# Long convolution and MLP on one core: v of the last two channel blocks fetched in the transform's layout, tables of the inverse transform read as a constant

## The chip, the core and the metric

The kernel runs on one core of one Trainium2 chip. The core has five engines with an instruction queue each: TensorE (PE, whose weight loads the profile shows as PEld), VectorE (DVE), ScalarE (ACT), GpSimd (POOL) and SyncE (SP, which here only issues DMAs). The metric is the device time of one execution in microseconds (us), as the median of several runs. Everything is float32; the MLP's products are done as sums of split operands.

## The reference

```python
mod = (silu(c) @ w_mod).reshape(1, 6, 1, 640)            # sa, ca, ga, sb, cb, gb
h  = layernorm(x) * (1 + ca) + sa                        # x is A_q, 2048 x 640
k_shift[s] = sum_t k[s - t] * shift_k[:, t]              # causal, 4 taps, by channel
kv = k_shift * v
y  = irfft(rfft(kv, 4096) * rfft(ssm_k, 4096))[:2048]    # long causal convolution by channel
y  = y + kv * ssm_D
x  = x + ga * (h * y)
h  = layernorm(x) * (1 + cb) + sb
x  = x + gb * (relu(h @ w1 + b1) ** 2 @ w2 + b2)         # 640 -> 1728 -> 640
```

## The kernel before

The 640 channels are worked in five blocks b = 0 to 4 of 128 channels. For each block the product x = k_shift * v is made with channels on the partitions, in four quarters h of 512 time steps: `kv_load` fetches 512 rows of k and of v (natural layout, time on the partitions) into one of the `KN` buffers; `kv_k` turns k round with four PE transposes (L223) and starts the sum of taps on ACT; `kv_s` adds the other taps on DVE (L235); `kv_v` turns v round with four transposes (L245) and issues the next `kv_load`; `kv_m` multiplies on DVE (L252) and stores the quarter to `kv_d` in DRAM (L253). When all four quarters are in DRAM, `load_x` (L200) reads them back in the transform's layout: partition (a, n) with a = 0 to 3 and n = 0 to 31, free axes g = 0 to 31 and i = 0 to 63, where the channel is 4g + a and the time step 64n + i. `load_h` (L192) reads ssm_k, the filter, in the same layout into the other half of the same tile `p`. `skip` adds ssm_D to the filter's first sample, so that the convolution gives y + kv * ssm_D; for block 0 it reads the row `d0` on POOL, for the others the table `dsm` on DVE (L139, `p<-p,dsm`).

The transform has these steps. `unit_a` (L360, tiles `pa`): a product along n, 16 units per block, the filter's eight first, then x's eight; ACT copies each unit to `a`. `spectrum` (L367): a product along i with the table `gb`, of the filter (tiles `h`, or `eh` in `early_h` for block 0) and of x. `front(b, j)`, j = 0 to 7: the two spectra, two DVE products of 128 x 512 (L136), two POOL sums (L142, L139). `back(b, j)`, j = 0 to 3 (L433, tiles `qp`): the inverse along i with the table `gi`, from the results of fronts 2j and 2j + 1. `unit_t` (L497) turns the result round, `unit_y` (L508) does the inverse along n and writes y to `up`. The gate and the residual follow on ACT (`prep_a`), DVE (`prep_m`, `gate`, `finish_near`) and POOL (`prep_p`, `finish_add`).

`gb` is read from DRAM as a constant. `gi` is made of it on the chip: `make_gi(i)`, i = 0 to 7, four PE transposes (L334) and a copy to `gi` by DVE or ACT; only its first half plane is read as a constant (L839).

The order is written out by hand. After a prologue (`kv_all`, the filter and x of block 0) there are steps: FS(b, 0 to 9), the spectrum phase of block b, in which eight fronts and four backs run and, at FS(b, 9), the first two `unit_a` of block b + 1; and GS(b, 0 to 17), the rest of block b, beside the other `unit_a` of block b + 1. `at(place, function)` hangs further work on a step: the kv quarters of block b in the steps of block b - 2, loads, the modulation rows (`part_load`, `part_scale`, `part_add`), LayerNorm statistics. `keep_order` fixes this order on every engine, so each queue is served strictly in the order of the program, SP's DMA queue too. An SP DMA also waits for the eighth DMA before it that uses the same semaphore. After block 4 the MLP runs (L680 to L784), and is not touched.

In the profiled execution the prologue lasts to 37.23 us, FS(0) to 64.0, GS(0) to 94.6, FS(1) to 121, GS(1) to 154.8, FS(2) to 178.5, GS(2) to 211.7, FS(3) to 236, and the MLP starts at about 309.

Of the kernel before, what the change touches and what calls it, by code (L numbers as in the profile page):

```python
# [30 lines left out]
def _constants():  # L31
    N = 4096
    n1 = np.arange(64)
    n2 = np.arange(32)
    m = np.arange(32)
    th = 2 * np.pi * ((n2[:, None] * m[None, :]) % 64) / 64
    cr, ci = np.cos(th), -np.sin(th)
    cr[:, 0] = 1.0
    ci[:, 0] = (-1.0) ** n2
    cw = np.zeros((4, 32, 2, 32, 4))  # L40
    for d in range(4):
        cw[d, :, 0, :, d] = cr
# [45 lines left out]
def ssm_mlp_kernel(  # L88
# [40 lines left out]
    def copy(eng, o, i):  # L129
        if eng is act:  # L130
            act.activation(o, i, AF.Copy)  # L131
        else:
            eng.tensor_copy(o, i)
# [45 lines left out]
    dve.memset(dsm, 0.0)  # L179
    tap = sb.tile([P, NB, 4], F32, tag="tap", name="tap")  # L180

    hsrc = ssm_k.rearrange("(g a) (n i) -> (a n) g i", a=4, i=64)
    xsrc = kv_d.rearrange("(g a) (n i) -> (a n) g i", a=4, i=64)
    pt = {}

    def p_tile(b):
        pt[b] = sb.tile([P, 2, DG, 64], F32, tag=f"S{b % 2}", name=f"p_{b}")

    def load_h(b, n=1):
        w = DG // n  # L190
        for i in range(n):
            sp.dma_start(  # L192
                pt[b][:, 1, i * w : (i + 1) * w],
                hsrc[:, b * DG + i * w : b * DG + (i + 1) * w, :],
            )

    def load_x(b, n=1):
        w = DG // n
        for i in range(n):
            sp.dma_start(  # L200
                pt[b][:, 0, i * w : (i + 1) * w],
                xsrc[:, b * DG + i * w : b * DG + (i + 1) * w, :],
            )
# [35 lines left out]
    def kv_v(b, h, tag="X"):  # L239
        t = kt[1] = ps.tile(  # L240
            [P, 512], F32, tag=tag, name=f"vt_{b}_{h}", bufs=4 if tag == "X" else 2
        )
        kn = KN[h % (4 if b == 0 else 2)]
        for j in range(4):
            pe.transpose(t[:, j * P : (j + 1) * P], kn[:, 1, j], ident)  # L245
        n = 4 * b + h + 2
        if 6 <= n < 4 * NB:
            kv_load(n)

    def kv_m(b, h):  # L250
        acc = KACC[h % 2] if b else K0[:, h]
        dve.tensor_mul(acc, kt[1], acc)  # L252
        sp.dma_start(kv_d[b * P : (b + 1) * P, h * 512 : (h + 1) * 512], acc)  # L253
# [70 lines left out]
    def load_gb():  # L324
        src = gb_d.rearrange("p (g r a f) -> p g r a f", g=16, r=2, a=2)
        for i in range(4):
            sp.dma_start(gb[:, 4 * i : 4 * i + 4], src[:, 4 * i : 4 * i + 4])
        sp.dma_start(gi[0:64, 0], gi0_d.rearrange("f (r n) -> f r n", r=2))

    def make_gi(i):  # L330
        t = ps.tile([P, 2, 2, P], F32, tag="T", name=f"git_{i}", bufs=2)
        for u in range(2):
            for r in range(2):
                pe.transpose(t[:, u, r], gb[:, 2 * i + u, r].rearrange("p a f -> p (a f)"), ident)  # L334
        if i == 0:
            copy(dve, gi[64:128, 0], t[64:128, 0])
            copy(dve, gi[:, 1], t[:, 1])
        else:
            copy(act if i % 2 else dve, gi[:, 2 * i : 2 * i + 2], t)
# [161 lines left out]
    def unit_y(b, g):  # L501
        if g % 2 == 0:
            ys[0] = ps.tile([P, 8, NL, 4], F32, tag="Y", name=f"y_{b}_{g}", bufs=2)
        y = ys[0]
        for i in range(4):
            for r in range(2):
                for h in range(2):
                    pe.matmul(  # L508
                        y[64 * h : 64 * h + 64, 4 * (g % 2) + i],
                        tss[g][:, i, 64 * r : 64 * r + 64],  # L510
                        ca[:, r, h],
                        start=(r == 0),
                        stop=(r == 1),
                    )
        if g % 2:
            uo = UPt[b][:, :, 16 * (g - 1) : 16 * (g + 1)].rearrange("p l (g d) -> p g l d", d=4)
# [331 lines left out]
    for a in range(4):  # L848
        pool.dma_start(
            dsm[32 * a : 32 * a + 1, :],  # L850
            ssm_D.rearrange("(o g a) -> a o g", a=4, o=1)[a],
        )
# [8 lines left out]
    def FS(b, j):  # L861
        return 28 * b + j
# [403 lines left out]
```

## Time and profile before

| | |
|---|---|
| median of 3 runs | 713.6 us (713.49 to 715.56) |
| profiled execution | 712.45 us |
| its span (first to last instruction) | 710.6 us |
| mean granted TensorE clock | 0.996 of full |
| instructions | 18542 |
| DVE busy | 339.1 us (48%) |
| ACT busy | 336.2 us (47%) |
| POOL busy | 297.3 us (42%) |
| DMA packets | 88403, 72.64 MB, of them 19392 under 512 B |

The profiled execution is one run of its own, so sums are made against 712.45 us, of which 1.85 us lie outside the span. A row of the timeline reads: start, length (of several merged instructions, from the first start to the last end), engine, line, operation, output<-inputs, count, and in brackets how long the engine sat idle before it and what released it. A row of the chain of waits reads: start, length, what. A row that groups instructions gives their count, busy time and mean length in ns. A row of busy time by window is explained where it is shown.

### The profile page before, as it was taken

How to read it: one execution, taken by the hardware profiler on the slowest of the kernel's cores; microseconds unless marked ns; L12 is line 12 of the kernel's file. 1: busy time of each engine (PE TensorE's matmuls, PEld its weight loads, DVE VectorE, ACT ScalarE, POOL GpSimd, SP SyncE). 2: the span in 40 equal slices, each digit the busy share in tenths (PEclk: the TensorE clock that was granted, in tenths of full speed). 3: DMA queues.
4: the chain of work that ended last, by engine and by line, in shares of the span. 5: the costliest groups of instructions: out<-in, count | busy, mean ns of one | idle time of the engine just before them, and what ended most of it. 6: DMA issues, size and time to landing. Idle time of an engine off the chain costs nothing.

```text
span 710.6 us, 18542 instructions
## 1 busy us (share of the span) xinstructions
PE 691.7 (97%) x7916; PEld 659.7 (93%) x7916; DVE 339.1 (48%) x667; ACT 336.2 (47%) x689; POOL 297.3 (42%) x343
## 2 busy tenths in 40 slices
PE   6899999999999999999999999999999999999997
PEld 5788898889899899789999999999999999999996
DVE  4355674775868679669831222222312313312313
ACT  3535565776884886557523323323333333233221
POOL 3033036157846969842532522422513415325213
PEclk9999999999999999999999999999999999999999
DMA  9787584869555464417320020020020100200101
GB/s 247 207 191 238 156 289 149 250 184 255 138 164 148 112 166 147 116 58 232 103 75 1 1 76 1 1 75 1 9 67 1 44 32 1 75 1 1 38 1 39
DMA packets 88403, 72.64 MB, mean 102 GB/s; under 512 B 19392, under 2 KB 74112, under 8 KB 88320
## 3 DMA queue, kind: packets, MB, share of 16 engines
q1 hardware_dynamic: 86176, 70.83, 34.8%
q8 instruction: 62, 1.02, 0.6%
q10 hardware_dynamic: 1888, 0.60, 0.4%
q14 instruction: 21, 0.17, 0.1%
q0 software_dynamic: 256, 0.01, 0.0%
HBM read 57.02 MB, written 14.42 MB: 101 GB/s over the span
## 4 chain that ended last, share of the span: by engine, by line
PE 90%; DVE 4%; ACT 2%; DMA 2%; issue 1%; POOL 1%; POOLq 0%; DVEq 0%; SPq 0%; ACTq 0%
PE acc L759 26%; PE h L689 25%; PE pa L360 9%; PE y L508 5%; PE qp L433 5%; PE x L367 5%; PE h L367 4%; PE t L497 3%; PE kt L223 1%; PE h L680 1%; PE vt L245 1%; PE xtp L654 1%; DVE KV L235 1%; PE gr L1035 1%; DMA d<-in_A_ssm_D_dram 1%
## 5 line engine op out<-in xcount | busy, mean ns | idle before, releaser
L136 POOL TENSOR_TENSOR mtmp<-mtmp 128x256 f32<-128x256 f32 x112 | 71.8, 641 | 242.2 <-ACT mtmp L721 232.5
L689 PE MATMUL h<-xt,w_S 128*128 128x256 f32 x1290 | 166.9, 281 | 0.2 <-DVE w_S L142 0.2
L689 PEld LDWEIGHTS h<-xt,w_S 128*128 128x128 f32 x1290 | 161.2, 190 | 0.4 <-DVE w_S L142 0.4
L759 PE MATMUL acc<-w_S,hring 128*128 128x320 f32 x960 | 156.8, 311 | 0.2 <-DVE hring L142 0.2
L142 DVE TENSOR_TENSOR hring<-mtmp,hring 128x256 fp32r<-128x256 f32 x112 | 65.1, 581 | 189.6 <-ACT hring L131 189.5
L759 PEld LDWEIGHTS acc<-w_S,hring 128*128 128x128 f32 x960 | 141.8, 188 | 0.7 <-DVE hring L142 0.7
L721 ACT ACTIVATE mtmp<-h,b1t 128x256 f32<-128x256 f32 x104 | 49.3, 474 | 176.6 <-PE h L689 173.6
L360 PE MATMUL pa<-wx,p 128*64 128x128 f32 x1280 | 82.8, 278 | 2.6 <-POOL p L139 1.8
L360 PEld LDWEIGHTS pa<-wx,p 128*64 128x64 f32 x1280 | 69.6, 138 | 9.6 <-issue 4.7
L131 ACT ACTIVATE hring<-mtmp 128x256 fp32r<-128x256 f32 x112 | 46.7, 417 | 45.7 <-POOL mtmp L136 44.2
L131 ACT ACTIVATE a<-pa 128x512 f32<-128x512 f32 x80 | 47.8, 602 | 27.9 <-PE pa L360 27.8
L136 DVE TENSOR_TENSOR wx<-x,wx 128x512 f32<-128x512 f32 x64 | 40.9, 681 | 19.3 <-PE x L367 10.1
L142 POOL TENSOR_TENSOR we<-wx 128x256 f32<-128x256 f32 x20 | 15.9, 794 | 73.5 <-DVE wx L136 69.8
L508 PE MATMUL y<-wx,wx 128*64 128x64 f32 x1280 | 45.0, 225 | 1.5 <-ACT wx L131 0.8
L508 PEld LDWEIGHTS y<-wx,wx 128*64 128x64 f32 x1280 | 41.7, 139 | 4.9 <-issue 2.6
L235 DVE SCALAR_TENSOR_TENSOR KV<-kt,tap,KV 128x511 f32<-128x511 f32 (+2 forms) x48 | 35.6, 743 | 19.0 <-ACT ktail L131 16.3
L139 POOL TENSOR_TENSOR wm<-wm,wm 128x640 f32<-128x640 f32 x20 | 32.0, 1602 | 29.5 <-ACT wm L308 29.3
L656 DVE TENSOR_SCALAR we<-xtp,cbs 128x256 f32<-128x256 f32 x35 | 19.0, 544 | 51.1 <-PE xtp L654 51.0
L367 PE MATMUL x<-a,gb 128*64 128x128 f32 x640 | 41.7, 273 | 0.7 <-ACT a L131 0.7
L131 ACT ACTIVATE q<-qp 128x512 f32<-128x512 f32 (+1 forms) x40 | 21.3, 584 | 36.1 <-PE qp L433 36.1
L367 PEld LDWEIGHTS x<-a,gb 128*64 128x64 f32 x640 | 35.9, 137 | 1.7 <-ACT a L131 0.9
L367 PE MATMUL h<-a,gb 128*64 128x128 f32 x512 | 34.1, 275 | 0.0
(145 smaller groups left out, 1040.5 us busy)
## 6 DMA issues: line engine op xcount, KB each, us to landing
wm<-in_w_mod_dram SPq DMA_DIRECT2D x25, 320.0 KB, 4.7
KV<-in_A_k_dram SPq DMA_DIRECT2D x20, 256.0 KB, 5.4
KV<-in_A_v_dram SPq DMA_DIRECT2D x20, 256.0 KB, 4.5
xp<-in_A_q_dram SPq DMA_DIRECT2D x5, 1024.0 KB, 7.5
out_dram<-x SPq DMA_DIRECT2D x14, 320.0 KB, 2.2
w1s<-in_B_w_dram SPq DMA_DIRECT2D x13, 320.0 KB, 3.7
w2s<-in_B_w_dram SPq DMA_DIRECT2D x13, 320.0 KB, 4.0
kv_d<-KV SPq DMA_DIRECT2D x16, 256.0 KB, 3.6
```

The lines of the kernel that those rows point to most:

```text
L131: act.activation(o, i, AF.Copy)
L136: eng.tensor_mul(o, a, b)
L139: eng.tensor_add(o, a, b)
L142: eng.tensor_sub(o, a, b)
L235: dve.scalar_tensor_tensor(o, x, tap[:, b, t : t + 1], o, op0=ALU.mult, op1=ALU.add)
L360: pe.matmul(t[64 * r : 64 * r + 64, u], w, cw[:, r], start=True, stop=True)
L367: pe.matmul(t[64 * a : 64 * a + 64, s + r], gb[:, g, r, a], AX[b][i][:, 2 * g + a], start=True, stop=True,)
L433: pe.matmul(t[a][:, u], gi[l, 4 * j + u, r], w[r][l, u % 2], start=(r == 0), stop=(r == 1),)
L508: pe.matmul(y[64 * h : 64 * h + 64, 4 * (g % 2) + i], tss[g][:, i, 64 * r : 64 * r + 64], ca[:, r, h], start=(r == 0), stop=(r == 1),)
L689: pe.matmul(hps[n, f][:m], WI[1, f][:, a, b], XT[n][:, x, b], start=(b == 0 and i == 0), stop=(b == NB - 1 and i == 2),)
L721: act.activation(r[:m], h[:m], AF.Relu, bias=b1t[:m, f : f + 1])
L759: pe.matmul(acc[2 * s + i], h[:, a, s * P : (s + 1) * P], w[:, y, i * 320 : (i + 1) * 320], start=(f == 0 and ti == 0), stop=(f == NF - 1 ...
```

## The change

Blocks 3 and 4 (`APART`) take another order of channels: partition (a, n), place g holds channel 32a + g in place of 4g + a. For them `kv_load` fetches k alone, `kv_v` and the DVE product of `kv_m` are gone, and what is stored to `kv_d` is the tap sum of k. v is fetched by `v_load` straight in the transform's layout into four buffers `VB` of 128 x 512 (i, g), that lie where the tap sums and the v halves of `KN` were: 16 DMAs per block, each 32 partitions x 16 steps x 32 channels, that is pieces of 128 B. `x_mul` multiplies them into x in place, four DVE products of 128 x 512 per block, in FS(2, 4 to 7) for block 3 and FS(3, 4, 5, 7, 8) for block 4. `load_x` and `load_h` of these blocks are four DMAs of 32 partitions in place of one. The write of y to `up` places its elements 32 apart in place of four side by side.

`gi` is read from DRAM whole, in four DMAs of 512 KB, and `make_gi` is gone. `early_h` 4 and 5 of block 0 move from FS(0, 0 and 1) into the prologue, 6 and 7 to FS(0, 0 and 1). Of the four `d0` loads two are now issued by ACT. The `dsm` loads become eight POOL DMAs in FS(0, 0 to 3), in place of four in the prologue. `skip` of blocks 1 and 3 moves from step 4 to step 8 of the spectrum phase before. The filter of block 2 is loaded at GS(0, 14) in place of FS(0, 2), that of block 3 at FS(2, 2) in place of FS(2, 0), and `load_xp` of block 1 at FS(2, 7) in place of FS(2, 1).

```diff
+    gb = gb.reshape(128, 16, 2, 2, 64).transpose(0, 1, 3, 2, 4)
+    gt = gb.transpose(3, 4, 1, 2, 0).copy()
+    gt[0, :, 0] = gi.reshape(2, 64, 128).transpose(1, 0, 2)
...
+        "gi": gt.reshape(128, 4096).astype(f),
...
+    APART = (3, 4)
+
+    def by_channel(src, b, i, dst):
+        w = dst.shape[1]
+        if b not in APART:
+            v = src.rearrange("(g a) (n i) -> (a n) g i", a=4, i=64)
+            sp.dma_start(dst, v[:, b * DG + i * w : b * DG + (i + 1) * w, :])
+            return
+        for a in range(4):
+            c = b * P + 32 * a + i * w
+            sp.dma_start(
+                dst[32 * a : 32 * a + 32],
+                src[c : c + w, :].rearrange("g (n i) -> n g i", i=64),
+            )
...
-        for w, src in ((0, k), (1, v)):
+        for w, src in ((0, k),) if b in APART else ((0, k), (1, v)):
...
     def kv_m(b, h):
         acc = KACC[h % 2] if b else K0[:, h]
-        dve.tensor_mul(acc, kt[1], acc)
+        if b not in APART:
+            dve.tensor_mul(acc, kt[1], acc)
         sp.dma_start(kv_d[b * P : (b + 1) * P, h * 512 : (h + 1) * 512], acc)
+    VB = [
+        t.rearrange("p (i g) -> p i g", g=DG)
+        for t in (KV[:, 0:512], KV[:, 512:1024], KV[:, 1536:2048], KV[:, 2560:3072])
+    ]
+
+    def v_load(b, j):
+        src = v.rearrange("(n i) d -> n i d", i=64)
+        for a in range(4):
+            c = b * P + 32 * a
+            sp.dma_start(
+                VB[j][32 * a : 32 * a + 32], src[:, 16 * j : 16 * j + 16, c : c + 32]
+            )
+
+    def x_mul(b, j):
+        x = pt[b][:, 0, :, 16 * j : 16 * j + 16]
+        mul(dve, x, x, VB[j].rearrange("p i g -> p g i"))
...
-    def make_gi(i):
...
+    def load_gi(i):
+        src = gi_d.rearrange("p (g r n) -> p g r n", g=16, r=2)
+        sp.dma_start(gi[:, 4 * i : 4 * i + 4], src[:, 4 * i : 4 * i + 4])
...
+                uo = UPt[b].rearrange("p l (d g) -> p g l d", d=4)[:, 4 * (g - 1) : 4 * (g + 1)]
...
-        pool.dma_start(
+        (pool if a % 2 else act).dma_start(
             d0[32 * a : 32 * a + 1, 0 : D - a], ssm_D[a:D].rearrange("(o d) -> o d", o=1)
...
-    for i in range(2):
-        make_gi(2 * i)
-        make_gi(2 * i + 1)
-        early_h(0, 2 * i)
-        early_h(0, 2 * i + 1)
+    for j in range(6):
+        early_h(0, j)
...
-        at(FS(b - 1, 4), skip, b)
+        at(FS(b - 1, 8 if b in (1, 3) else 4), skip, b)
...
+    for a in range(4):
+        at(FS(0, a), load_dsm, a)
+    for j in range(2):
+        at(FS(0, j), early_h, 0, 6 + j)
...
-    at(FS(0, 2), load_h, 2)
+    at(GS(0, 14), load_h, 2)
...
-        at(FS(2, 0) if b == 3 else GS(2, 1), load_h, b)
+        at(FS(2, 2) if b == 3 else GS(2, 1), load_h, b)
+
+    put_v(3, [FS(2, i) for i in (0, 0, 1, 1)], [FS(2, i) for i in (4, 5, 6, 7)])
+    put_v(4, [FS(3, i) for i in (0, 0, 1, 1)], [FS(3, i) for i in (4, 5, 7, 8)])
...
-    at(FS(2, 1), load_xp, 1)
+    at(FS(2, 7), load_xp, 1)
```

More of the change, by code (lines that the diff above doesn't have):

```diff
@@ L105, in ssm_mlp_kernel @@
     gb_d: bass.AP,
-    gi0_d: bass.AP,
+    gi_d: bass.AP,
     out: bass.AP,
@@ L180, in ssm_mlp_kernel @@
     tap = sb.tile([P, NB, 4], F32, tag="tap", name="tap")
-    hsrc = ssm_k.rearrange("(g a) (n i) -> (a n) g i", a=4, i=64)
-    xsrc = kv_d.rearrange("(g a) (n i) -> (a n) g i", a=4, i=64)
     pt = {}
@@ L191, in load_h @@
         for i in range(n):
[L192 to L195, printed above, removed]
+            by_channel(ssm_k, b, i, pt[b][:, 1, i * w : (i + 1) * w])
     def load_x(b, n=1):
@@ L199, in load_x @@
         for i in range(n):
[L200 to L203, printed above, removed]
+            by_channel(kv_d, b, i, pt[b][:, 0, i * w : (i + 1) * w])
     def kv_load(i):
@@ L245, in kv_v, with kv_next @@
             pe.transpose(t[:, j * P : (j + 1) * P], kn[:, 1, j], ident)
+        kv_next(b, h)
+    def kv_next(b, h):
         n = 4 * b + h + 2
@@ L322, in ssm_mlp_kernel @@
     gi = sb.tile([P, 16, 2, P], F32, tag="S6", name="gi")
[L324 to L328, printed above, removed]
-    def make_gi(i):
[L331 to L339, printed above, removed]
+    def load_gi(i):
+        src = gi_d.rearrange("p (g r n) -> p g r n", g=16, r=2)
+        sp.dma_start(gi[:, 4 * i : 4 * i + 4], src[:, 4 * i : 4 * i + 4])
     AX, QT = {}, {}
@@ L515, in unit_y @@
         if g % 2:
-            uo = UPt[b][:, :, 16 * (g - 1) : 16 * (g + 1)].rearrange("p l (g d) -> p g l d", d=4)
+            if b not in APART:
+                uo = UPt[b][:, :, 16 * (g - 1) : 16 * (g + 1)].rearrange("p l (g d) -> p g l d", d=4)
+            else:
+                uo = UPt[b].rearrange("p l (d g) -> p g l d", d=4)[:, 4 * (g - 1) : 4 * (g + 1)]
             if b < NB - 1:
@@ L809, in load_h0 @@
     def load_h0(i):
-        sp.dma_start(pt[0][:, 1, 8 * i : 8 * i + 8], hsrc[:, 8 * i : 8 * i + 8, :])
+        by_channel(ssm_k, 0, i, pt[0][:, 1, 8 * i : 8 * i + 8])
         skip(0, 8 * i, 8 * i + 8)
@@ L838, in ssm_mlp_kernel, with load_dsm @@
     load_gb(3)
-    sp.dma_start(gi[0:64, 0], gi0_d.rearrange("f (r n) -> f r n", r=2))
     kv_load(4)
+    load_gi(0)
     kv_load(5)
+    load_gi(1)
     load_h(1)
-    for i in range(2):
-        make_gi(2 * i)
-        make_gi(2 * i + 1)
-        early_h(0, 2 * i)
-        early_h(0, 2 * i + 1)
[L848 to L851, printed above, removed]
+    load_gi(2)
+    load_gi(3)
+    for j in range(6):
+        early_h(0, j)
+    def load_dsm(a):
+        pool.dma_start(
+            dsm[32 * a : 32 * a + 1, 0:96],
+            ssm_D[0 : 3 * P].rearrange("(o g a) -> a o g", a=4, o=1)[a],
+        )
+        pool.dma_start(
+            dsm[32 * a : 32 * a + 1, 96:].rearrange("o (c g) -> o c g", g=DG),
+            ssm_D[3 * P :].rearrange("(o c a g) -> a o c g", o=1, a=4, g=DG)[a],
         )
@@ L879, in put_kv, with put_v @@
             at(p4[0], kv_k, b, h, tags[h])
+            if b in APART:
+                at(p4[1], kv_s, b, h)
+                at(p4[1], kv_next, b, h)
+                at(p4[2], kv_m, b, h)
+                continue
             for i, fn in zip(p4[1:], (kv_s, kv_v, kv_m)):
                 at(i, fn, b, h)
+    def put_v(b, ld, mu):
+        for fn, p4 in ((x_mul, mu), (v_load, ld)):
+            for j, i in enumerate(p4):
+                at(i, fn, b, j)
     for b in range(1, NB):
-        at(FS(b - 1, 4), skip, b)
-    for j in range(4):
-        at(FS(0, j // 2), make_gi, 4 + j)
-        at(FS(0, j), early_h, 0, 4 + j)
+        at(FS(b - 1, 8 if b in (1, 3) else 4), skip, b)
[3 more added lines that the diff above has]
+        at(FS(0, j), early_h, 0, 6 + j)
     put_kv(1, [
```

3 lines of the change are left out of this document (1 added, 2 removed).

## The prediction

> **What bounds the kernel now.** I read the page's busy shares and chain first, then busy time by stage, then the rows inside the stages that change. On the page:
>
> ```profile
> PE 691.7 (97%) x7916; PEld 659.7 (93%) x7916; DVE 339.1 (48%) x667; ACT 336.2 (47%) x689; POOL 297.3 (42%) x343
> PE 90%; DVE 4%; ACT 2%; DMA 2%; issue 1%; POOL 1%; POOLq 0%; DVEq 0%; SPq 0%; ACTq 0%
> ```
>
> TensorE is busy for 97% of the span and is 90% of the chain that ends last. A TensorE instruction taken out is therefore worth its time, unless the stage that it stood in has another limit close behind. The busy times by stage show that. Columns: window, its length, busy time of PE, PEld, DVE, ACT, POOL, then granted clock, DMA share, GB/s.
>
> ```profile
> 37.23:64.00 26.77, 26.25 (x385) 22.96 (x385) 17.27 (x30) 9.36 (x18) 11.76 (x18) 1.00 0.78 197
> 121.00:154.81 33.81, 32.98 (x570) 28.68 (x566) 23.23 (x52) 25.87 (x46) 9.28 (x6) 1.00 0.72 205
> 154.81:178.52 23.71, 23.71 (x390) 21.89 (x389) 13.48 (x24) 15.51 (x33) 17.09 (x21) 1.00 1.03 258
> 178.52:211.65 33.13, 32.63 (x586) 29.60 (x586) 27.82 (x53) 28.15 (x60) 21.64 (x16) 1.00 0.54 155
> 211.65:236.05 24.40, 24.40 (x424) 23.18 (x420) 17.60 (x32) 13.06 (x24) 16.98 (x22) 1.00 0.44 121
> ```
>
> These are FS(0), GS(1), FS(2), GS(2) and FS(3). PE is full in all of them. In GS(2), ACT (28.15 of 33.13) and DVE (27.82) are near.
>
> Before 37.23 something else is the limit. The chain in order of time (start, length, what):
>
> ```profile
> 3.51 4.71 DMA d<-in_A_ssm_D_dram
> ...
> 19.86 2.37 DVE kacc L235 x6
> 23.04 2.37 DMA kv_d<-kacc
> ...
> 29.34 7.22 PE pa L360 x128
> ```
>
> The start hangs on d0, and from 19.86 to 29.34 on the product of block 0 and its way through DRAM. TensorE waits there.
>
> **The change part by part.** 64 transposes leave PE: 32 that made `gi` (L334, 8 groups of 4) and 32 of v for blocks 3 and 4 (L245, 8 groups). That they are gone is certain from the order of the instructions. Their price is the distance of starts:
>
> ```profile
> 38.26 0.66 PE L334 MATMUL git<-ident,gb 128*128 128x128 f32 x4
> 38.84 1.09 PE L367 MATMUL eh<-a,gb 128*64 128x128 f32 x16
> ...
> 41.38 1.04 PE L367 MATMUL eh<-a,gb 128*64 128x128 f32 x16
> 42.35 1.09 PE L334 MATMUL git<-ident,gb 128*128 128x128 f32 x8
> 43.79 0.66 PE L223 MATMUL kt<-ident,KV 128*128 128x128 f32 x4 [0.35 <-DVE gi L133]
> ...
> 70.05 0.66 PE L497 MATMUL t<-ident,q 128*128 128x128 f32 x4
> 70.64 1.09 PE L360 MATMUL pa<-wx,p 128*64 128x128 f32 x16
> ...
> 125.78 0.66 PE L245 MATMUL vt<-ident,KV 128*128 128x128 f32 x4
> ...
> 126.80 1.09 PE L360 MATMUL pa<-wx,p 128*64 128x128 f32 x16
> ```
>
> A `gi` group takes 38.84 - 38.26 = 0.58 us, an `early_h` 42.35 - 41.38 = 0.97 at most (0.9 taken, as the two beside each other run closer). A v group stands ahead of a t group: both take 1.02, a t group alone 0.59, so it is worth 0.43.
>
> *Prologue.* Four `gi` groups go and two more `early_h` come, all inside the wait that ends at 29.34: worth 0. But d0 now comes through two POOL and two ACT issues in place of four on POOL. The last POOL issue started at 3.51; now it is the second, two issues earlier, at 0.535 each (the L849 row below): 1.1. The chain starts with it: **+1.1**. At the least it is 0, if the first piece of ssm_k, or ACT's two issues, is what comes last then.
>
> *FS(0).* Four `gi` groups (two alone, 1.16, and two in 42.35 to 43.79, 1.44 with the wait) and two `early_h` (1.8) leave PE: 4.4. What is late next is in these rows:
>
> ```profile
> L849 POOL DMA_DIRECT2D dsm<-in_A_ssm_D_dram x4: 528/535/557, 16.1 to 17.7; - x4
> ...
> 40.50 0.73 POOL L139 TENSOR_TENSOR we<-wx 128x256 f32<-128x256 f32 x1
> ...
> 41.40 0.28 POOL L414 COPY we<-wx 1x128 f32<-1x128 f32 x1
> ...
> 57.73 0.74 DVE L235 SCALAR_TENSOR_TENSOR KV<-kt,tap,KV 128x511 f32<-128x511 f32 x1
> ...
> 59.68 1.97 PE L360 MATMUL pa<-wx,p 128*64 128x128 f32 x32
> ...
> 60.22 1.28 DVE L136 TENSOR_TENSOR wx<-x,hs 128x512 f32<-128x512 f32 x2
> ```
>
> That last row is the eighth front's product. The dsm loads, in four DMAs at 16.1 in an idle POOL, become eight, two behind each of the fronts 0 to 3, 0.535 each. So POOL has 2 x 0.73 + 2 x 0.535 = 2.5 us per front. From 41.7 (end of L414) fronts 1, 2 and 3 are ready at 44.2, 46.7 and 49.3, and the second `qp`, which needs front 3, starts at 49.3 (52.64 before). Then come 2.0 of it, 0.6 of kt and 0.9 of x: x of front 6 is there at 52.8. Behind that DVE has in order front 6 (1.3), the taps of k, quarter 1 of block 1 (60.22 - 57.73 = 2.5), front 7 (1.3), and now skip(1), moved from FS(0,4) to FS(0,8): 58.2. PE's next instruction, pa of block 1, needs skip(1) and could have run at 56.1. It starts at 58.2 in place of 59.68, and with `qp` 3 behind it the stage ends 1.9 earlier (62.1 for 64.0): **+1.9** of the 4.4. The eight DMAs' landing (about 49.3 + 1 + 6) is no later than that. The 2 MB of `gi` on SP's queue stand ahead of the ssm_k of block 1, and lie in the 27 us at 197 GB/s above; they are due at the `qp`s from 44.2 on: 0, and 0 to 2 if they are late.
>
> *GS(1) and GS(2).* Eight v groups: 8 x 0.43 = 3.5. Eight DVE products go too, and 8 of SP's 256 KB loads. In GS(2), 33.1 - 1.7 = 31.4 remain for ACT's 28.15, which is 90% with waits in order: I take off 0.5: **+3.0** (bounds 1 and 3.5).
>
> *FS(2).* Four products of v, 24 DMAs of 32 partitions (x 4, v 16, ssm_k 4; before 2 DMAs) and skip(3) at FS(2,8) meet here:
>
> ```profile
> 150.13 1.54 DVE L235 SCALAR_TENSOR_TENSOR KV<-ktail,tap,KV 128x3 f32<-128x3 f32 x1
> 154.37 0.38 SPq L253 DMA_DIRECT2D kv_d<-KV  x1
> 158.99 0.68 SPq L200 DMA_DIRECT2D p<-kv_d  x1
> 160.12 3.47 SPq L192 DMA_DIRECT2D p<-in_A_ssm_k_dram  x1
> ...
> 171.11 0.22 DVE L139 TENSOR_TENSOR p<-p,dsm 128x32 f32<-128x32 f32 x1 [3.40 <-issue]
> ...
> 175.67 1.27 DVE L136 TENSOR_TENSOR wx<-x,wx 128x512 f32<-128x512 f32 x2
> ...
> 176.62 1.97 PE L360 MATMUL pa<-wx,p 128*64 128x128 f32 x32
> 161.00:169.00 8.00, 8.00 (x140) 7.54 (x138) 3.29 (x6) 4.89 (x10) 6.08 (x8) 1.00 1.13 223
> ```
>
> x and ssm_k, 1 MB each in pieces of 256 B, took from 158.99 to 171.11 (skip(3) waited for the second): 12.1 us. At the 223 GB/s of the last row a load is 4.7 of it, and 2.7 are start and landing. The store waited until 154.37 for the loads ahead of it in the queue and for the product of v; now it can go when the taps end (150.13 + 1.54 = 151.67) and the queue has issued one load, at about 152.2, and x 2.2 us earlier than before, at 156.8. Between the two stands v, 8192 pieces of 128 B. No row has such a piece. Below, at equal bytes per us, it takes 4.7; above, at equal pieces per us, 9.4. I take 7. ssm_k lands at 156.8 + 12.1 + 7 = 175.9 (173.6 to 178.3). SP's 24 issues, at 0.4 each (row 154.37), are under that.
>
> DVE: products with both inputs in SBUF run from
>
> ```profile
> 214.95 0.68 DVE L136 TENSOR_TENSOR up<-up,KV 128x512 f32<-128x512 f32 x1
> ...
> 218.85 2.29 DVE L136 TENSOR_TENSOR up<-up,KV 128x512 f32<-128x512 f32 x1
> ```
>
> 0.68 to 2.29; I take 0.9, nearer the free one, because POOL has gaps between its pairs. The strided v operand is priced as these rows; doubled it would add 0.7. The 3.4 us that DVE lost ahead of 171.11 pay for the first three. Front 7 stays at 175.67; behind it are 1.27, the fourth product 0.9, one more of the gate's rows (0.7) and skip (0.2): 178.7. Block 3's pa wants it at 176.62: a new wait of **-2.0** (bounds 0 and -5). What is queued behind skip(3) on DVE, the gate of block 0, loses nothing that PE waits for.
>
> *FS(3).* The same four products; skip(4) stays early and x, v have from about 212 to 226. Front 7 is late by 0.2: **-0.2**. The strided writes of block 3's and 4's y are priced at 0; the four in GS(3) have 7 us of free DVE, and doubling the last two of block 4 would cost 0.7.
>
> *Clock.* A wait of TensorE has cost a second time here:
>
> ```profile
> 285.00:288.40 3.40, 1.88 (x26) 1.33 (x23) 1.17 (x3) 3.37 (x9) 3.40 (x4) 1.00 0.00 0
> 288.60:292.00 3.40, 3.40 (x32) 3.07 (x31) 3.37 (x5) 2.31 (x4) 3.40 (x3) 0.50 0.00 0
> ...
> 288.41 2.64 PE L497 MATMUL t<-ident,q 128*128 128x128 f32 x12 [1.29 <-ACT q L131]
> ```
>
> After 3.4 us in which PE was busy for 1.88, the granted clock was 0.50 for 3.4 us. Twelve transposes took 2.64 there, against 3 x 0.59 = 1.8; with the y behind them I put such a stretch at 1.3. The change makes three waits of about 2 us (before 29.34 minus 1.1, before skip(1), before skip(3)). I charge one stretch: **-1.3** (bounds 0 and -3.9). [...]
>
> Sum: 1.1 + 1.9 + 3.0 - 2.0 - 0.2 - 1.3 = **2.5 us less**. The profiled execution took 712.45 (span 710.6 and 1.85 around it), so 709.95 by that; it ran 1.15 under the median of 713.6, so I name 713.6 - 2.5 = **711.1**.
>
> **The rivals.** *The clock stays full.* For it: the clock stands at 1.00 in all five stages quoted first, short waits and all. Against: the rows at 285 to 292. Gain 3.8: 709.8.
>
> *No new wait.* If both skips are in time and ACT keeps up, all is gained: 1.1 + 4.4 + 3.5 = 9.0: 704.6. For it is PE at 97%; against it are the two DVE queues counted above.
>
> *Slower: the ssm_k of block 3 is late behind v.* It is one queue, and pa of block 3 waits for its end. The time follows what a piece of 128 B costs: at 1.15 ns (a piece of 256 B: 4.7 us / 4096) DVE is still the later one. The gain is gone when skip(3) comes 2.5 later, v taking about 12 us (1.5 ns a piece); slower by over 0.3% begins near 14.5. At twice a 256-B piece, 18.8, ssm_k lands at 187.7, pa waits 11 in place of 2, and the kernel takes about 720. For it: the pieces are half the size and the DMAs cover 32 partitions. Against: fewer bytes per piece should not take longer. [...]
>
> *Others are the limit already.* ACT in GS(1) and GS(2) and DVE in FS(0) give back the rest: gain 0 to 1, 713. For it: 28.15 busy on ACT; against: PE has hardly an idle row in those stages.
>
> **How the numbers follow.** About 0.3%, 2.1 us, is what a measurement of this kernel can tell from no change. Chances: forecast 0.40 (own range 709.6 to 712.6), clock full 0.20, no new wait 0.12, v late 0.15, others the limit 0.13. Faster: 0.23 of the forecast's 0.40, 0.18 of 0.20, all 0.12: 0.53. Slower: 0.13 of v late, 0.03 of the rest: 0.16. Same: 0.31. The range from 706.0 to 716.0 leaves out most of "no new wait" and the costly end of "v late", some 0.18.
>
> **What would show it.** No L334, and 48 transposes on v's line. pa of block 0 near 28.3. pa of block 1 ended by DVE's skip, about 2 us idle; pa of block 3 the same, or a DMA of ssm_k if v is slow. Products of v at 0.7 to 1.2 us. A 0.5 clock behind one of these waits. The prediction is wrong if ssm_k of block 3 lands after 179, if GS(1) and GS(2) shrink by under 2 us together, or if the d0 loads do not move the start.

## The result and the profile after

| | before | after |
|---|---|---|
| median | 713.6 us (711.99 to 715.56, 5 runs) | 719.8 us (717.87 to 721.65, 5 runs) |
| profiled execution, its span | 712.45, 710.6 us | 719.8, 718.0 us |
| mean granted clock | 0.996 | 0.989 |

The ratio is 1.0083, with a 95% interval of 1.0055 to 1.0111: the change made the kernel slower by 6.2 us, where 2.5 less was forecast. The page's busy line and its chain by engine:

```profile
PE 687.6 (96%) x7852; PEld 655.8 (91%) x7852; DVE 344.2 (48%) x662; ACT 334.1 (47%) x685; POOL 302.1 (42%) x345
PE 84%; DVE 4%; DMA 3%; ACT 3%; SPq 2%; issue 2%; POOL 1%; DVEq 0%; POOLq 0%; ACTq 0%
```

PE has 4.1 us less to do, as meant (64 transposes fewer), but is 84% of the chain in place of 90%: DMA and SP's queue now stand in it. Where, is read from the stages. A stage is taken from the start of its first row on PE to the start of the next one's: FS(b) from its first spectrum, GS(b) from the second group of `pa` behind the spectra.

| stage | before | after | difference | forecast |
|---|---|---|---|---|
| start of FS(0) | 37.23 | 36.42 | -0.8 | -1.1 |
| FS(0) | 26.77 | 25.54 | -1.2 | -1.9 |
| GS(0) and FS(1) | 57.84 | 57.84 | 0 | 0 |
| GS(1) | 32.97 | 32.10 | -0.9 | -3.0 with GS(2) |
| FS(2) | 25.69 | 35.64 | **+9.9** | +2.0 |
| GS(2) | 31.21 | 29.32 | -1.9 | |
| FS(3) | 24.34 | 27.53 | **+3.2** | +0.2 |
| GS(3) | 27.55 | 27.54 | 0 | 0 |
| FS(4) to the MLP | 45.49 | 44.33 | -1.2 | 0 |
| MLP | 401.5 | 401.7 | +0.2 | 0 |
| half clock, in no stage | | | | +1.3 |
| sum | | | +7.4 | -2.5 |

All that was removed is there; two stages lose more than all of it. The busy times by window show FS(2), GS(2) and FS(3), then the two stretches at half clock and what went ahead of the first (columns as in the prediction):

```profile
151.90:187.54 35.64, 28.25 (x421) 26.01 (x420) 24.23 (x31) 17.13 (x36) 26.81 (x26) 0.86 0.92 169
187.54:216.86 29.32, 28.81 (x540) 26.05 (x540) 19.77 (x46) 26.19 (x55) 13.42 (x10) 1.00 0.74 177
216.86:244.39 27.53, 25.56 (x423) 23.44 (x419) 22.55 (x36) 13.17 (x24) 20.27 (x22) 1.00 0.76 145
...
53.25:56.66 3.41, 1.18 (x16) 0.81 (x14) 3.41 (x10) 1.08 (x2) 1.14 (x3) 1.00 1.00 353
56.66:60.07 3.41, 3.41 (x34) 3.08 (x30) 0.33 (x1) 0.64 (x2) 1.20 (x2) 0.50 0.85 211
...
176.12:186.36 10.24, 5.12 (x46) 4.79 (x48) 6.77 (x6) 1.72 (x4) 8.96 (x7) 0.50 0.97 227
```

PE is idle for 7.4 of FS(2)'s 35.6 us, and 10.24 us of it have half the clock. The timeline names the waits:

```profile
28.52 7.21 PE L380 MATMUL pa<-wx,p 128*64 128x128 f32 x128 [1.73 <-DMA p<-kv_d]
...
56.45 3.53 PE L380 MATMUL pa<-wx,p 128*64 128x128 f32 x32 [2.23 <-DVE p L142]
...
181.24 3.68 PE L380 MATMUL pa<-wx,p 128*64 128x128 f32 x32 [7.23 <-DVE p L142]
```

Both waits that were forecast behind a skip are there: 2.2 us for skip(1), and 7.2 in place of 2.0 for skip(3). The group of 32 `pa` takes 3.5 and 3.7 us, where it took 1.97. What was ahead of skip(3) is seen on SP's queue and on DVE:

```profile
155.13 3.10 SPq L201 DMA_DIRECT2D p<-kv_d  x4
158.28 12.11 SPq L280 DMA_DIRECT2D KV<-in_A_v_dram  x16
170.44 4.14 SPq L201 DMA_DIRECT2D p<-in_A_ssm_k_dram  x4
...
175.93 1.02 DVE L139 TENSOR_TENSOR p<-p,KV 128x512 f32<-128x512 f32 x1
176.87 1.22 DVE L139 TENSOR_TENSOR KV<-KV,g1row 128x512 f32<-128x512 f32 x1
180.38 0.81 DVE L142 TENSOR_TENSOR p<-p,dsm 128x32 f32<-128x32 f32 x1 [2.28 <-DMA p<-in_A_ssm_k_dram]
```

v holds the queue for 12.1 us, ssm_k lands 25.3 us after x was issued (12.1 before: 171.11 - 158.99), and skip(3) waits for it with DVE idle. In FS(3) the waits are POOL's:

```profile
231.54 1.05 DVE L139 TENSOR_TENSOR p<-p,KV 128x512 f32<-128x512 f32 x1
231.67 1.51 POOL L145 TENSOR_TENSOR we<-wx 128x256 f32<-128x256 f32 x1 [1.29 <-PE qp L453]
...
239.61 2.58 DVE L139 TENSOR_TENSOR p<-p,KV 128x512 f32<-128x512 f32 x2
239.67 1.61 POOL L142 TENSOR_TENSOR wx<-wx 128x256 f32<-128x256 f32 x1
241.24 1.54 POOL L145 TENSOR_TENSOR wx<-wx 128x256 f32<-128x256 f32 x1
241.33 0.94 PE L453 MATMUL qp<-wx,gi 64*128 64x128 f32 x12 [0.69 <-POOL wx L142]
```

A sum of POOL that lies beside a product of v takes 1.5 to 1.6 us, against 0.73 with none beside it, and PE's `qp` waits for it. So the prediction's rival "ssm_k of block 3 late behind v" came about, with a second loss that no part of the prediction had.

### The profile page after: what moved, and what is told of

The parts are those of the page before. It is cut to its first block, busy times and chain, and to the rows that moved or that the text cites. A ratio compares the mean times of both kernels' runs of the same rounds, so it can differ in the third digit from the quotient of the medians.

```text
span 718.0 us, 18468 instructions
## 1 busy us (share of the span) xinstructions
PE 687.6 (96%) x7852; PEld 655.8 (91%) x7852; DVE 344.2 (48%) x662; ACT 334.1 (47%) x685; POOL 302.1 (42%) x345
## 3 DMA queue, kind: packets, MB, share of 16 engines
q8 instruction: 62, 1.02, 0.6%
## 4 chain that ended last, share of the span: by engine, by line
PE 84%; DVE 4%; DMA 3%; ACT 3%; SPq 2%; issue 2%; POOL 1%; DVEq 0%; POOLq 0%; ACTq 0%
PE acc L782 26%; PE h L712 25%; PE pa L380 10%; PE y L528 5%; PE qp L453 4%; PE x L387 3%; PE t L517 3%; PE h L387 3%; SPq L280 2%; PE kt L234 2%; PE h L703 1%; PE xtp L677 1%; DMA p<-in_A_ssm_k_dram 1%; PE vt L256 1%; DMA kv_d<-KV 1%
## 5 line engine op out<-in xcount | busy, mean ns | idle before, releaser
L744 ACT ACTIVATE mtmp<-h,b1t 128x256 f32<-128x256 f32 x104 | 49.3, 474 | 177.5 <-PE h L712 174.5
L380 PE MATMUL pa<-wx,p 128*64 128x128 f32 x1280 | 86.3, 285 | 12.2 <-DVE p L142 9.5
L380 PEld LDWEIGHTS pa<-wx,p 128*64 128x64 f32 x1280 | 72.8, 143 | 19.5 <-DVE p L142 9.9
```

The source lines that it names most:

```text
L380: pe.matmul(t[64 * r : 64 * r + 64, u], w, cw[:, r], start=True, stop=True)
L744: act.activation(r[:m], h[:m], AF.Relu, bias=b1t[:m, f : f + 1])
```

## The experiments

The kernel before ran beside each group, with medians from 712.4 to 714.3; ratios are against it. Four groups asked in turn: which part loses, which step of it, whether its order can be mended, and what sets the pace of the fetches. Stage times are of one profiled execution of each kernel, and executions of one kernel differ in half clock: the changed kernel's five runs have mean clocks from 0.986 to 0.995, and the one at 0.995 is the fastest (717.87 us).

**Each part alone.** The tables part (v's part undone: `APART = ()`, skip(3), load_h and load_xp back):

```diff
-    APART = (3, 4)
+    APART = ()
-    put_v(3, ...)
-    put_v(4, ...)
```

> The tables part alone: gi as a constant, d0 on two engines, skip(1) at FS(0,8), dsm fetched by POOL in FS(0), ssm_k of block 2 in GS(0); v of blocks 3 and 4 is again transposed and multiplied as in the kernel before. Theory A (the loss is all in FS(2) and FS(3), from v): the profile shows the first x at 36.4, pa of block 1 after a wait of about 2.2 us at 56.5, and from there on the kernel before 2.0 us earlier: span about 708.6, 2 us under the kernel before (1 more if the half-clock stretch near 288 is absent as in the changed kernel). Theory B (the wait for skip(1) and its half clock cost on as well): equal to the kernel before or slower, 713 to 716.

Measured: 709.79 us, ratio 0.9952 (0.9933 to 0.9971). FS(2) took 25.93, FS(3) 24.36. Theory A holds for this part, with the wait for skip(1) in it (56.15, 2.23 idle).

The v part (`make_gi`, d0, dsm, skip(1) and load_h(2) as before; the rest as after):

> The v part alone: blocks 3 and 4 with v fetched whole, four products each, skip(3) at FS(2,8); gi, d0, dsm, skip(1) as in the kernel before. Theory A: FS(2) 35 to 36 us against 25.7, FS(3) 27.5 against 24.3, GS(1) and GS(2) together 2.8 shorter: about 10 us slower than the kernel before, span about 721. Theory B (both parts cost): at most 4 us slower, 717.

Measured: 721.42 us, ratio 1.0125 (1.0101 to 1.0148). FS(2) 35.09, FS(3) 29.08 with half clock in it (0.96 over the stage), GS(1) 32.02, GS(2) 29.32. The loss is v's alone, and the two parts nearly add: -2.6 and +9.0 make +6.4; the whole change has +6.2.

**Which step.** The changed kernel without the eight products, then without v's fetches:

```diff
-        for fn, p4 in ((x_mul, mu), (v_load, ld)):
+        for fn, p4 in ((v_load, ld),):
```

> The changed kernel with the products by v of blocks 3 and 4 left out, so these blocks are computed without v; v is still fetched. Theory A (in FS(2) the DMA queue is late, in FS(3) the products slow POOL): pa of block 3 still waits for skip(3), that for ssm_k at about 180, some 6 to 7 us idle and the half clock behind it, so FS(2) keeps 34 to 36 us; in FS(3) POOL's pairs are back at 0.73 us and the stage at 24.4, 3 us less. Time about 716.5. Rival C (DVE's queue of products holds skip(3)): the wait is under 1 us, FS(2) about 25, time 706 or less.

Measured: 716.79 us, 1.0058 (1.0034 to 1.0081). FS(2) 33.50, with 5.76 us of wait; FS(3) 25.54:

```profile
174.46 0.67 DVE L139 TENSOR_TENSOR KV<-KV,g1row 128x512 f32<-128x512 f32 x1
179.75 0.38 DVE L142 TENSOR_TENSOR p<-p,dsm 128x32 f32<-128x32 f32 x1 [4.62 <-DMA p<-in_A_ssm_k_dram]
```

DVE now stands idle for 4.6 us, and skip(3) comes 25.4 us after x was issued (154.35), as with the products (25.3): they don't hold it, rival C falls. In FS(3) the products are worth 2.0 of the 3.2 us; most of POOL's sums are back at 0.73. The other 1.2 are the queue again. Three loads of the gate's weights are issued behind v's sixteen DMAs, at 232.26, 16.9 us into the stage; before, the last was out at 6.6. ACT waits for one in its order, and so its copy for the eighth front comes at 21.1 us of the stage in place of 19.2, and that front's product on DVE 1.2 later:

```profile
235.75 0.83 ACT L341 ACTIVATE wm<-wm,sg 128x640 f32<-128x640 f32 x1 [1.73 <-DMA wm<-in_w_mod_dram]
```

```diff
-        for fn, p4 in ((x_mul, mu), (v_load, ld)):
+        for fn, p4 in ((x_mul, mu),):
```

> The changed kernel with the fetches of v for blocks 3 and 4 left out; the eight products stay and read what lies in the four buffers, so the output is not the reference's. Theory A: ssm_k of block 3 is issued 12 us earlier and lands by 170; what remains late is the fourth product on DVE, at about 177, so pa of block 3 waits about 3 us instead of 7.2, with 3.4 us of half clock behind it instead of 10; FS(2) 29 us instead of 35.6, FS(3) still 27.5. Time about 713. Rival C: FS(2) keeps its 35 us, time 719 to 720. If v's fetches and not the products cost FS(3) its 3 us, FS(3) is 24.4 and the time 710.

Measured: 716.32 us, 1.0049 (1.0032 to 1.0066), FS(2) 31.37, FS(3) 27.51 (so there the products alone cost the whole 3.2, and the fetches show only without them). The wait was 3.35 us, for skip(3) at 177.23, which stood behind the fourth product and a row of the gate on DVE. That is theory A's queue (the total came out 3 above its 713: its figure for FS(2), 29, left out a wait of 0.83 us for the gate's sums on POOL and most of the half clock). So v's fetches are worth 3.9 of the 7.2, DVE's order the other 3.4.

**Can the order be mended?** First ssm_k of block 3 ahead, in GS(1), and skip(3) back at step 4:

```diff
-        at(FS(b - 1, 8 if b in (1, 3) else 4), skip, b)
+        at(FS(b - 1, 8 if b == 1 else 4), skip, b)
-        at(FS(2, 2) if b == 3 else GS(2, 1), load_h, b)
+        at(GS(b - 2, 8) if b == 3 else GS(2, 1), load_h, b)
```

> The changed kernel with ssm_k of block 3 fetched at GS(1,8), ahead of x and v, and skip(3) back at FS(2,4). Theory A (skip(3) came late because ssm_k stood behind v's pieces on SP's queue): what is left is DVE's order, the fourth product ending near 177 as without v's fetches: pa of block 3 waits about 3 us, one half-clock stretch behind it, FS(2) about 31.4 in place of 35.6; time 715 to 716. Rival D (v's pieces are late for the products themselves): the wait stays at 6 us or more, ended by a product, FS(2) 34 or more, time 719.

Measured: 719.99 us, 1.0078 (1.0063 to 1.0093). FS(2) fell to 27.58, no wait ahead of `pa` (it starts at 178.99, before the fourth product at 179.50, so it needs the skip, not the product). But GS(1) took 35.28, GS(2) 31.77, FS(3) 29.05: nothing is left of the gain. In GS(1) the loads of the gate's weights now stand behind ssm_k, ACT waits for them in its order, and PE for the copy behind them:

```profile
148.73 0.83 ACT L341 ACTIVATE wm<-wm,sg 128x640 f32<-128x640 f32 x1 [1.57 <-DMA wm<-in_w_mod_dram]
...
150.82 0.83 ACT L341 ACTIVATE wm<-wm,sg 128x640 f32<-128x640 f32 x1 [0.78 <-DMA wm<-in_w_mod_dram]
151.56 0.58 ACT L134 ACTIVATE wx<-t 128x512 f32<-128x512 f32 x1
...
152.19 1.15 PE L528 MATMUL y<-wx,wx 128*64 128x64 f32 x32 [3.47 <-ACT wx L134]
```

Then ssm_k ahead of v inside FS(2):

```diff
-        at(FS(2, 2) if b == 3 else GS(2, 1), load_h, b)
+        at(FS(2, 0) if b == 3 else GS(2, 1), load_h, b)
-    put_v(3, [FS(2, i) for i in (0, 0, 1, 1)], [FS(2, i) for i in (4, 5, 6, 7)])
+    put_v(3, [FS(2, i) for i in (0, 0, 1, 1)], [FS(2, i) for i in (6, 7, 8, 9)])
```

> The changed kernel with only the order on SP's queue and DVE altered in FS(2): ssm_k of block 3 issued at FS(2,0) ahead of v, skip(3) at FS(2,5), the four products at FS(2,6) to FS(2,9). Theory A (TensorE waits for skip(3), that for ssm_k behind v; the products are needed only by the second group of pa, some 4 us later): no wait before pa of block 3 over 1 us, the clock 1.00 there, FS(2) 26 to 27, GS(1) still 32.1 (the gate's weights aren't pushed back, as they were with ssm_k in GS(1)): time 710 to 711. Rival G (x, v and ssm_k are one sum on the queue, whatever their order): now v lands last and the second group of pa waits for the fourth product, 3 to 6 us, FS(2) 30 or more, time 716 or more.

Measured: 719.14 us, 1.0067 (1.0041 to 1.0093). FS(2) 27.53 and GS(1) 31.98 as theory A had it, but GS(2) 34.95 (clock 0.95, one half-clock stretch in it): neither theory. On DVE not a gap is left from 170.08 to 199; the products with both inputs in SBUF, beside a row of 7.54 us for four on POOL (178.76), take 1.57 to 2.13 us (the gate's rows before: 0.68 and 0.70 at 172.45 and 175.04, up to 1.77 in GS(2)), and the taps of k come late:

```profile
170.08 0.22 DVE L142 TENSOR_TENSOR p<-p,dsm 128x32 f32<-128x32 f32 x1 [2.99 <-DMA p<-in_A_ssm_k_dram]
...
178.14 1.57 DVE L139 TENSOR_TENSOR p<-p,KV 128x512 f32<-128x512 f32 x1
179.64 1.77 DVE L139 TENSOR_TENSOR KV<-KV,g1row 128x512 f32<-128x512 f32 x1
181.34 2.13 DVE L139 TENSOR_TENSOR p<-p,KV 128x512 f32<-128x512 f32 x1
183.38 3.47 DVE L139 TENSOR_TENSOR up<-up,KV 128x512 f32<-128x512 f32 x2
186.78 2.31 DVE L246 SCALAR_TENSOR_TENSOR KV<-kt,tap,KV 128x511 f32<-128x511 f32 x3
```

To tell DVE from the queue, the same kernel without products (blocks 3 and 4 again without v):

> The kernel with ssm_k ahead of v, with the eight products left out, so blocks 3 and 4 are computed without v; all fetches stay. Theory H (two limits stood one behind the other: ssm_k's place on the queue, and DVE, which the products and their collisions with POOL fill from 170 to 200): both are gone, FS(2) 26 to 27, GS(2) 29.3, FS(3) 25.5, span about 707, time 708 to 709.5, some 10 us under the same kernel with products. Rival I (what came back in GS(2) is the queue again: the gate's weights and k behind v): GS(2) stays at 33 or more and the time at 714 or more.

Measured: 712.58 us, 0.9977 (0.9965 to 0.9988). FS(2) and GS(2) together, from the four kernels:

| us of FS(2) and GS(2) | with products | without |
|---|---|---|
| ssm_k behind v | 64.96 | 62.82 |
| ssm_k ahead of v | 62.48 | 57.87 |

Before they took 56.90. Theory H holds in kind: the queue's place is worth 5.0 without products but 2.5 with them, the products 2.1 behind the queue and 4.6 when it no longer hides them. Half clock is part of these sums: 10.24 us of it in 64.96, 6.83 in 62.82, 3.41 in 62.48 and none in 57.87 (clocks of 0.86 and 0.90 over FS(2), 0.95 over GS(2), and 1.00). In FS(0) a stretch of 3.41 costs 1.6 (25.51 us with it, 23.94 without; rows in the last section), so by that price the 4.6 is 3.0 without it. Theory H's sum was too good by 3 to 4.5 us: GS(2) stayed at 31.99, where PE waits 2.25 us for DVE's taps, and FS(3) at 27.32, with a half-clock stretch in it. GS(2)'s 29.32 in the changed kernel was lent to it: there the gate's rows `up<-up,KV` run on DVE at 182.81, ahead of GS(2) (187.54); with ssm_k ahead of v and products they run at 183.38, inside it (179.72).

v whole for block 4 alone, and the place of skip(1):

```diff
-    APART = (3, 4)
+    APART = (4,)
```

> The changed kernel with v fetched whole for block 4 alone; block 3 as in the kernel before. Theory A: FS(2) is back at 25.7 to 26; GS(1) loses its 0.9; FS(3) 27.5, GS(2) 29.3 to 30: span about 709.5, time 711 to 712. Rival: if the delay is not v's in FS(2), FS(2) stays over 30 and the time at 717 or more.

Measured: 714.74 us, 1.0007 (0.9986 to 1.0028); FS(2) 25.69, GS(2) 30.79, FS(3) 27.49. FS(2)'s loss is block 3's; block 4 saves 0.4 in GS(2) and loses 3.2 in FS(3). The median is 3 above the forecast, its profiled run (span 709.7) is at it.

```diff
     for a in range(4):
-        at(FS(0, a), load_dsm, a)
+        load_dsm(a)
-        at(FS(b - 1, 8 if b in (1, 3) else 4), skip, b)
+        at(FS(b - 1, 8 if b == 3 else 4), skip, b)
```

> The changed kernel with the eight dsm loads issued in the prologue and skip(1) at FS(0,4), ahead of block 1's taps on DVE. Theory E (skip(1)'s place alone costs the 2.2 us of wait and the 1.6 of half clock behind it): no wait before pa of block 1 but a few tenths, clock 1.00 there, FS(0) 21.8 in place of 25.5, span 714.3, time 716. Rival F (another step is late in its place, the eighth front on DVE behind the taps): a wait of 1 to 2 us ended by DVE or POOL, FS(0) 23.5 or more, time 718.

Measured, with the calls of `load_dsm` in the prologue: 718.06 us, 1.0054 (1.0035 to 1.0072), FS(0) 21.93: theory E for the stage; the time is 2 above it, with FS(3) at 28.21. With the tables part alone (dsm in four loads as before):

> The tables part alone (v as in the kernel before), with dsm fetched in the prologue in four loads and skip(1) at FS(0,4). Theory E: FS(0) 21.8, everything else as with the tables part alone: span about 704.5, time about 706, 6 to 7 us under the kernel before. Rival F: FS(0) 23.5 or more, or the gain given back in GS(0): 708 to 710.

Measured: **706.55 us, 0.989 (0.9873 to 0.9906)**, the best kernel of the study. The two groups that stood apart by a wait now follow each other, and the clock is 1.00 until the end (0.998 in the mean):

```profile
54.17 0.66 PE L256 MATMUL vt<-ident,KV 128*128 128x128 f32 x4
54.76 1.97 PE L380 MATMUL pa<-wx,p 128*64 128x128 f32 x32
56.66 2.38 PE L453 MATMUL qp<-wx,gi 64*128 64x128 f32 x32
```

Two kernels put v back on top of it, with ssm_k ahead of v: for block 3 alone (here the buffers of block 3's v also overwrite the first two quarters of block 4's, so that block 4 is computed with other values of v), and for both:

> Tables part with dsm in the prologue and skip(1) at FS(0,4), and v fetched whole for block 3 alone, with ssm_k ahead of v and the products at FS(2,6) to FS(2,9). Theory A: FS(0) 21.9, GS(1) 32.1, FS(2) 26 to 27, the rest as in the kernel with the tables part and skip(1) early (706.55): 705.5 to 706.5. Rival G: FS(2) 30 or more, 709 to 711.

> As the kernel before this one, with v fetched whole for block 4 as well, in the places of the changed kernel. Theory A: GS(2) 29.3 in place of 32.2, FS(3) 27.5 in place of 24.4 (POOL's pairs beside the products): 705.5 to 707, no better than the version without v for block 4 by more than 0.5. Rival: the half clock comes on top in FS(3), 708.

Measured: 710.72 us, 0.9951 (0.9934 to 0.9967), and 715.87 us, 1.0027 (1.0009 to 1.0046). Both expectations missed by 4 to 9 us: GS(2) took 34.07 and 35.53, with waits of 2.0 and 2.5 us for DVE's taps as above, and with half clock in it (0.97 and 0.90 over the stage). v fetched whole for block 3 costs 4.2 us on top of the best kernel, for both blocks 9.3.

**What sets the pace of the fetches.** Half as many pieces of v, of 256 B, with the same bytes and number of DMAs:

```diff
-                VB[j][32 * a : 32 * a + 32], src[:, 16 * j : 16 * j + 16, c : c + 32]
+                VB[j][32 * a : 32 * a + 32].rearrange("p (i t) g -> p i (t g)", t=2),
+                src[:, 16 * j : 16 * j + 16 : 2, min(c, 576) : min(c, 576) + 64],
```

> The changed kernel with v's DMAs as many and of the same bytes, but each in 256 pieces of 256 B in place of 512 of 128 B; it fetches other places of v, so the output is not the reference's. If the number of pieces sets the pace: v passes in 5 to 6 us in place of 11, SP's 16 issues (0.49 each) take 8, ssm_k lands near 176 and skip(3) follows DVE's queue at 177 to 178: a wait of 3.5 to 4.5 us in place of 7.2, one half-clock stretch, FS(2) 31.5 to 32.5, time about 716. If the bytes, or the number of DMAs, set it: FS(2) stays at 35 or more, time 719 to 720.

Measured: 717.65 us, 1.0056 (1.0037 to 1.0075), FS(2) 32.82, wait 4.57. That looks like the first case, but x was issued at 153.44 there, 1.7 sooner; from x's issue to skip(3) (178.12) it is 24.7 us against 25.3. The size of the pieces is worth 0.6 us.

x and ssm_k in one DMA each (`if b not in APART` in `by_channel` replaced by `if True`):

> The changed kernel with x and ssm_k of blocks 3 and 4 fetched by one DMA each in the old order of channels, and v as in the changed kernel, so that channels don't match and the output is not the reference's; bytes are the same. From x's issue to skip(3) the changed kernel took 25.3 us: 16 for x and ssm_k in four DMAs of 32 partitions (12.1 in the kernel before, in one DMA each) and 9.2 for v. Theory J (the split form of x and ssm_k is the term that was taken at nothing): skip(3) 3.5 to 4 us sooner after x's issue, 21.5, the wait before pa of block 3 down to some 3.5 us, where DVE's queue is the later, FS(2) 31 to 32, time 716. Theory K (v alone, or the number of bytes on the queue): 25 us as before, FS(2) 35, time 719 to 720.

Measured: 716.35 us, 1.0028 (1.0015 to 1.0041), FS(2) 33.33. From x's issue (152.17) to skip(3) (175.99) 23.8 us: 1.4 less, not 4. Theory J falls as the main cause, K is nearer. Half of v's DMAs issued by ACT:

```diff
-            sp.dma_start(
+            (act if a % 2 else sp).dma_start(
                 VB[j][32 * a : 32 * a + 32], src...
```

> The changed kernel with every second DMA of v (8 of a block's 16) issued by ACT in place of SP. Theory L (v is paced by SP's issue: 64 KB each 0.53 us, while the DMA share falls to 0.57 to 0.95): ssm_k of block 3 is issued 5 to 7 us sooner, and the time from x's issue to its landing falls from 25.3 to 20 to 22 us; pa of block 3 waits 3 to 4.5 us in place of 7.2, less what ACT's eight issues of 0.5 (in front of its copies for fronts 1 and 2) cost at the start of FS(2), up to 2 us: FS(2) 32 to 34, time 717 to 719. Theory M (the DMA engines or the pieces set it): 25 us again, FS(2) 35 or more, time 720 or more.

Measured: 721.09 us, 1.0107 (1.0086 to 1.0128). ssm_k was issued 15.2 us after x (154.27 and 169.45), against 15.3 in the changed kernel: theory L falls, SP's own rate is not the limit. FS(2) was 32.74 all the same, but DVE was the later (skip(3) followed a gate's row without a gap) and no half clock followed the wait ahead of `pa`, 2.26 us; one stretch of 3.41 lay at 173.6, behind a wait of 2.41 for the gate's sums on POOL. So it doesn't bear out L. These rows show v's fetch in the changed kernel (166 to 170), x's packets ahead of it (160), and ssm_k's behind it (174):

```profile
160.00:162.00 2.00, 2.00 (x38) 1.88 (x38) 0.55 (x1) 0.87 (x2) 1.67 (x3) 1.00 1.35 159
...
166.00:168.00 2.00, 2.00 (x38) 1.88 (x36) 2.00 (x3) 1.24 (x3) 2.00 (x2) 1.00 0.85 136
168.00:170.00 2.00, 1.84 (x16) 1.06 (x12) 2.00 (x3) 2.00 (x6) 2.00 (x2) 1.00 0.57 86
...
174.00:176.00 2.00, 0.01 (x2) 0.00 (x0) 2.00 (x4) 1.96 (x5) 0.25 (x1) 1.00 1.36 164
```

Before, x and ssm_k passed at 223 GB/s with a share of 1.13. Now they pass at some 160 with a share of 1.35, and v at 86 to 136 with a share of 0.57 to 0.95. What paces v's 64 KB DMAs stays open: not its pieces, not SP alone, nor a semaphore (SP's queue shows no wait ahead of them). No run fetched v in fewer DMAs, or in DMAs of more than 32 partitions.

## Why the prediction was wrong, point by point

- **Prologue, +1.1.** Right in kind: 0.8 (28.52 for 29.34). With the new d0 loads FS(0) starts at 35.8 to 37.1 in fourteen kernels and at 38.7 in one; with the old ones at 37.2 and 37.8. The new ones spread over 1.3 us, more than the 0.8.
- **FS(0), +1.9.** The wait for skip(1) came as worked out, 2.23 for "about 2", but 1.75 earlier (56.45 for 58.2): POOL's dsm issues did not hold PE, the second `qp` began at 47.01, not 49.3. The half clock behind it took 1.6 back. Net 1.2. The remedy, skip(1) where it was, is worth another 3.6 (21.93).
- **GS(1) and GS(2), +3.0.** Measured 2.8, and yet the reason was off: not ACT but DVE is next in GS(2). Where v of block 3 is fetched whole and PE no longer waits for skip(3), GS(2) takes 31.8 to 35.5 (the longest with half clock in it), no less than the 31.21 of before. So 1.9 of the 2.8 came only with FS(2)'s delay, and that the sum fits is luck.
- **FS(2), -2.0: the step that failed, in three places.** First, PE: the working had it want skip(3) at 176.62, its place of before, though the terms ahead had just brought it forward. It was ready at 174.0 (181.24 - 7.23); what PE had gained up to there was turned into waiting, since the fetch did not come sooner with it: 2.6. Second, the fetches. The term said 12.1 us for x and ssm_k and 7 for v. With ssm_k ahead of v, x and ssm_k took 16.1 (issue at 153.99, skip(3) at 170.08), and their eight DMAs held the queue for 10.8 us and landed 6.4 us after issue in the median, against 11.0 and 6.8 in the kernel without v's fetches; the forecast priced them as if four DMAs of 32 partitions were one of 128. v then adds 9.2, inside its bounds. x left at 155.13, 1.7 sooner than worked out. 175.9 - 1.7 + 4.0 + 2.2 = 180.4, and skip(3) ran at 180.38, past the 179 that the prediction named as the sign of being wrong, and 1.9 behind the 178.5 at which the forecast has it start. Third, skip(3) took 0.81 us, not 0.2, with POOL beside it (3.70 us from 178.64), which is 0.6 more. The forecast's wait (178.7 less 176.62, 2.1) + 2.6 + 1.9 + 0.6 is the wait of 7.2. The split alone doesn't explain the 4.0: in the run with x and ssm_k whole only 1.4 came back, and v held the queue for 14.95 us in place of 12.11. The 25.3 us are measured only as a sum, and the forecast had no row for such a DMA. "SP's 24 issues are under that" was wrong too: with v they held the queue for 19.4 us.
- **DVE in FS(2), 178.7.** Near, by luck: without v's fetches skip(3) started at 177.2 where the forecast has 178.5. Front 7's products came 1.7 sooner there (173.94 for 175.67), and what stands between them and skip(3) took 0.5 more. v's products took 1.0 to 1.6, not 0.9.
- **FS(3), -0.2.** Measured -3.2. The products were priced on DVE alone; what they do to POOL was left out, though the rows of 0.68 and 2.29 us were quoted for DVE's side of the same collision. So was what v's fetches do to the gate's weights behind them on the queue.
- **Clock, -1.3.** One stretch was charged; there were two, of 3.4 us (1.6) and 10.24 us: from 181.24 to the next group PE needed 6.30 us against 3.88, so 2.4. The stretch near 288 of before was absent, 1.2 back. Net -2.8.
- **The rivals.** "Slower: ssm_k late behind v" had 0.15 and about 720: the place and nearly the time, but not its price: that hung on the size of a piece, which is worth 0.6 us. `pa` of block 3 started at 181.24, 2.5 us behind the forecast's 178.7, which is where that rival has the gain just gone; the wait of 11 us behind its 720 did not come (7.2). PE's lead, the clock and FS(3) made up the rest, so that the time is near 720 is luck. "Others are the limit already" held in GS(2), for DVE.

Side by side the rows of both engines came out longer: a sum of POOL that takes 0.73 us took 1.5 beside a product of v (233.15 and 231.67 in the changed kernel), and the products of v took from 1.02 (175.93 there) to 2.13 us on DVE (181.34 in the kernel with ssm_k first). What the two share, no run shows. A second issuing engine was no help to ssm_k: 15.2 us after x with half of v's DMAs on ACT, for 15.3.

## What to carry to other kernels

Work taken off the bounding engine is priced on every queue that it lands on, and on what that queue's engine collides with: here 32 transposes (2.8 us) became products on DVE that doubled POOL's sums beside them (0.73 to 1.5 us), and fetches ahead of others that were due on the same queue. Time gained ahead of a fetch that does not come sooner is no gain but a wait (2.6 us in FS(2)), so each due time is to be moved forward with the terms ahead of it. Before a small step is put later in an engine's order, ask who waits for it: one skip moved back, with the loads of its table in the prologue again, was worth 3.2 us (709.79 to 706.55).

## What the runs showed of the hardware that was not expected

The same wait of 2.2 us ahead of `pa` of block 1 cost a half-clock stretch in seven kernels and none in four, in one profiled execution of each. FS(0) of the tables part alone (clock 0.93), and of the kernel with ssm_k first and no products (1.00):

```profile
36.13:61.64 25.51, 23.28 (x337) 21.03 (x337) 15.89 (x28) 7.02 (x14) 13.67 (x22) 0.93 0.97 268
```

```profile
35.86:59.80 23.94, 21.71 (x337) 19.59 (x337) 15.90 (x28) 7.02 (x14) 15.79 (x26) 1.00 0.95 266
```

The price of the stretch of 3.41 us is 1.6 us there (25.51 for 23.94), with PE busy all through it in the changed kernel (56.66 to 60.07). The stretches seen are 3.41 us long, or two or three times that: 10.24 at 176.12 in the changed kernel, 6.83 by the clock of FS(2) (0.90 over 33.50 us) in the one without products. The changed kernel's two start 119.46 us apart, 35.0 times a third of the longer one. PE was not idle for the whole of the 3.41 us ahead of the first (53.25 to 56.66), but busy for 1.18. Why the same wait cost a stretch in some kernels and none in others was not shown.
